# Two infini-attention and two Fourier layers: score blocks of 384 and 128 columns in one PSUM bank, value products merged, a 136-column memory update and direct row copies

## The chip, the cores and the metric

The kernel runs on one core of one Trainium2 chip. The metric is device time in microseconds (us) of one execution; of several runs the median counts. The engines are TensorE (PE in the profile, its weight loads PEld), VectorE (DVE), ScalarE (ACT), GpSimd (POOL) and SyncE (SP), which here only issues DMAs.

## The reference

Sequence 2048, width 512, 32 heads of 16, four segments of 512. Four residual layers alternate:

```python
def _A_ref(x, wq, wk, wv, wo, beta):          # q, k, v: x @ w, by head and segment
    for s in range(4):
        p = softmax(qs @ ks.T * scale + causal_mask);  a_dot = p @ vs
        a_mem = (phi(qs) @ M) / (phi(qs) @ z + 1e-6)
        outs.append(g * a_mem + (1 - g) * a_dot)
        M = M + phi(ks).T @ vs;  z = z + phi(ks).sum()
    return concat(outs) @ wo
def _B_ref(x, ...):                            # real part of a 2-D Fourier transform
    a, b = x @ dft_hid_re.T, x @ dft_hid_im.T
    return dft_seq_re @ a - dft_seq_im @ b
x = x + _A_ref(layernorm(x), ...); x = x + _B_ref(layernorm(x), ...)   # twice
```

## The kernel before

Large products are done as three fp16 products of split numbers (high and low half). A **group** is eight heads of one segment; there are 32 (`NGRP`): two layers, four segments, four groups. For each group, generators emit these steps:

- `s_p` and `s_v` project q, k and v. `t_split` splits q and k into halves (`hl`) and carries them as rows into the staging tiles `qst` and `kst`: two DMAs write `hl` to a DRAM tile `d`, four read it back with the rows rearranged. There are two such tiles of each (`NR` = 2), used in turn, so the rows of group i wait until the exponentiated scores of group i-2 are issued, `gate(("ST", i - NR))`.
- `s_x` computes scores to find each row's maximum. A head pair `p`, with its two halves `a` on the upper and lower 64 rows of the array at once, has four blocks of 128, 256, 384 and 512 columns (causal: block `t` has `128 * (t + 1)`). A **step** fills one PSUM bank for each half. `t_max` reduces each block on VectorE.
- `s_st` computes the scores again, transposed and with the maximum subtracted through two extra rows. `t_sel` exponentiates a whole bank on ScalarE into a tile `pt` and cuts the diagonal on GpSimd.
- `s_av` multiplies by the values. Four head pairs write four 32-row strips of one bank, in 32-column array strips side by side. The stationary operand is 32 fp32 columns of the value tile `vt`.
- `s_mem` reads the memory `macc` and updates it: `phk` (128 by 128, fp32) times `v[:, t]`, 192 fp32 columns (for each head pair the values of one head, 16 ones, the values of the other). `t_merge` joins both parts, `s_o` projects with `wo`; then `s_ab` and `s_f` do the Fourier layer, nearly all of it 128x512 fp16 products.

The order on every engine is set when the program is built. A list scheduler, `Plan`, keeps a cost model of the engines and always takes the generator that can go on first, corrected by a table of biases (`LEAN`). Every `yield need(engine, ...)` is a point where it may turn to another generator; instructions between two such points stay together. An engine then executes its instructions strictly in that order. TensorE works in three shapes: the whole array (m), two halves of 64 rows (h, the scores) and four strips of 32 columns (v, the value products). `t_warm` fills gaps that the planner foresees with dummy products of `onesb`. All instructions have the line of one helper (L272), so tiles tell them apart: `b` is a PSUM bank, `w`, `g`, `m` are work tiles, `y` the residual sum, which is also the staging area for weights at the start.

## Time and profile before

| | |
|---|---|
| median of three runs | 1695.57 us (1693.65 to 1700.11) |
| profiled execution, its own time | 1699.92 us |
| its span, first to last instruction | 1698.2 us |
| TensorE busy | 1662.3 us |
| VectorE, ScalarE, GpSimd busy | 1036.8, 872.3, 810.3 us |
| mean granted TensorE clock | 0.989 |

The span is what the trace covers; 1.7 us of the profiled time lie around it. A busy TensorE is not one that streams: the profile counts a product from its start to its modelled end, so the time in which one product drains and none streams is busy as well.

### The profile page before, as it was taken

The numbers are of one execution on the slowest core, as the hardware profiler recorded it, in microseconds if no ns is written. First come the engines' busy times: TensorE is split into PE (matmuls) and PEld (weight loads), VectorE is DVE, ScalarE is ACT, GpSimd is POOL, SyncE is SP. The second block draws the span as 40 slices with busy tenths as digits, with TensorE's granted clock in tenths as the row PEclk, the third lists the DMA queues.
The fourth block names the chain that finished last, engine by engine and source line by source line (L and its number), as shares of the span: only waits on it lengthen the run. The fifth ranks groups of instructions, "written<-read, shape, count | busy, mean of one in ns | idle before, by whom it ended". The sixth has DMA issues, their size and how long they took to land.

```text
span 1698.2 us, 32247 instructions
## 1 busy us (share of the span) xinstructions
PE 1662.3 (98%) x11145; PEld 734.7 (43%) x11145; DVE 1036.8 (61%) x3262; ACT 872.3 (51%) x1480; POOL 810.3 (48%) x1445
## 2 busy tenths in 40 slices
PE   8889999999999999999999999999999999999999
PEld 4344344444444344444544444443444444444444
DVE  8784865778677786635768558546575765433221
ACT  5487577755656666535376754655455325312000
POOL 4376556575565556634255644635454415322000
PEclk9789999999999999999999999999999999999999
DMA  7546545655357432525746663543435322131423
GB/s 182 147 116 178 128 132 159 172 142 152 94 148 208 126 119 84 189 56 196 193 148 187 182 179 90 132 116 98 140 91 149 105 85 76 57 125 38 143 70 123
DMA packets 208629, 222.92 MB, mean 131 GB/s; under 512 B 104520, under 2 KB 127048, under 8 KB 208464
## 3 DMA queue, kind: packets, MB, share of 16 engines
q1 hardware_dynamic: 208464, 220.85, 45.8%
q8 instruction: 88, 1.44, 0.4%
q14 instruction: 77, 0.63, 0.1%
HBM read 137.40 MB, written 61.87 MB: 117 GB/s over the span
## 4 chain that ended last, share of the span: by engine, by line
PE 77%; DVE 9%; ACT 5%; issue 4%; DMA 3%; POOL 2%; SPq 1%; ACTq 0%; DVEq 0%; POOLq 0%
PE b L272 77%; ACT w L272 4%; DVE junk L272 4%; SPq L272 1%; DVE w L272 1%; POOL w L272 1%; DMA w<-w 1%; DMA w<-x 1%; DVE m L272 1%; DVE mx L272 1%; DVE y L272 1%; DVE bst L272 0%; DVE cam L272 0%; DMA w<-in_cs_dram 0%; DVE pmax L272 0%
## 5 line engine op out<-in xcount | busy, mean ns | idle before, releaser
L272 PEld LDWEIGHTS <-w 128*128 128x128 f16 x5056 | 467.8, 98 | 612.8 <-issue 101.1
L272 PE MATMUL b<-w,w 128*128 128x512 f16 x3072 | 708.5, 380 | 1.7 <-DVE mx L272 0.8
L272 ACT ACTIVATE w<-b,fac 128x512 f32<-128x512 f32 (+1 forms) x728 | 419.2, 655 | 176.3 <-PE b L272 175.8
L272 DVE CUSTOM_DVE_ANT_0 junk<-b,cmask 128x128 bf16<-128x128 f32 (+3 forms) x1024 | 436.3, 483 | 71.6 <-PE b L272 71.1
L272 POOL TENSOR_TENSOR w<-w,w 128x512 f16<-128x512 f32 (+1 forms) x294 | 347.5, 1187 | 247.1 <-ACT w L272 223.6
L272 POOL TENSOR_SCALAR_AFFINE_SELECT w<-w 128x128 f32<-128x128 f32 (+2 forms) x704 | 237.0, 350 | 202.7 <-ACT w L272 194.1
L272 DVE SCALAR_TENSOR_TENSOR y<-b,fyu,y 128x512 f32<-128x512 f32 x200 | 148.9, 745 | 235.6 <-PE b L272 235.2
L272 ACT ACTIVATE w<-w,csc 128x512 f16<-128x512 f32 (+1 forms) x256 | 180.1, 720 | 41.5 <-DVE csc L272 32.8
L272 PE MATMUL b<-g,w 128*128 128x512 f16 x768 | 183.1, 383 | 3.2 <-DMA g<-w 0.8
L272 PE MATMUL b<-wd,w 128*128 128x512 f16 x768 | 176.8, 379 | 0.1
L272 PE MATMUL b<-w,vt 128*32 128x512 f32 (+3 forms) x2048 | 172.4, 449 | 1.9 <-POOL w L272 1.1
L272 ACT ACTIVATE w<-b 128x512 f16<-128x512 f32 x128 | 75.9, 596 | 189.4 <-PE b L272 179.3
L272 DVE SCALAR_TENSOR_TENSOR w<-b,w 128x512 f16<-128x512 f32 x128 | 87.6, 687 | 120.3 <-ACT w L272 118.7
L272 ACT ACTIVATE w<-w 128x512 f16<-128x512 f32 (+1 forms) x137 | 86.5, 632 | 90.1 <-DVE w L272 87.9
L272 PE MATMUL b<-kst,qst 48*128 48x128 f16 (+3 forms) x1024 | 117.5, 304 | 6.3 <-DVE mx L272 3.2
L272 PE MATMUL b<-qst,kst 50*128 50x512 f16 (+3 forms) x1024 | 115.8, 302 | 5.5 <-DVE mx L272 2.2
L272 PE MATMUL b<-w,g 128*128 128x128 f16 x1536 | 96.3, 221 | 0.0
L272 PEld LDWEIGHTS <-g 128*128 128x128 f16 x1536 | 89.6, 99 | 12.7 <-issue 7.8
L272 DVE STREAM_TRANSPOSE m<-b 128x512 f32<-128x512 f32 x112 | 75.6, 698 | 31.1 <-PE b L272 30.7
L272 PEld LDWEIGHTS b<-w,vt 128*32 128x32 f32 x2048 | 54.8, 110 | 87.7 <-issue 48.2
L272 PE MATMUL b<-wo,w 128*128 128x512 f16 x384 | 89.1, 379 | 0.0
L272 PEld LDWEIGHTS <-kst 50*128 50x128 f16 x1024 | 37.3, 94 | 111.7 <-issue 105.2
(105 smaller groups left out, 1019.3 us busy)
## 6 DMA issues: line engine op xcount, KB each, us to landing
w<-in_cs_dram SPq DMA_DIRECT2D x128, 256.0 KB, 3.5
cc<-w SPq DMA_DIRECT2D x128, 256.0 KB, 3.2
w<-cc SPq DMA_DIRECT2D x128, 256.0 KB, 3.1
w<-w SPq DMA_DIRECT2D x96, 256.0 KB, 3.5
d<-w SPq DMA_DIRECT2D x128, 128.0 KB, 2.5
w<-in_x_dram SPq DMA_DIRECT2D x32, 256.0 KB, 3.6
qst<-d SPq DMA_DIRECT2D x64, 128.0 KB, 2.7
kst<-d SPq DMA_DIRECT2D x64, 128.0 KB, 3.3
```

What stands on the lines that cost most here:

```text
L272: r = f(*args, **kw)
```

## The change

Five things, and a new order as their result.

1. **Steps.** The blocks of 384 and of 128 columns of a head pair share a bank, so a group has ten steps for each of its two score passes, not eleven. The order of steps is 512 first, then pairs of 256 and the shared ones (maxima, `"abc"`), or 512, shared, 256 (second pass, `"acb"`).
2. **Value products.** The products of the 384 and of the 128 columns follow each other without a scheduling point between them. The value tile is laid out as `[row, t, d, head]`, so the 32 stationary columns lie 8 fp32 numbers apart.
3. **Update.** The moving operand of the memory update is `v[:, t, :17]`: 128 value columns and 8 of ones, 136 for 192. The mask product reads it in two strided pieces.
4. **Rows.** For the first three groups, and whenever the tile's earlier user is already issued, q and k rows go straight from `hl` to the staging tile, by six DMAs. Three of the first groups have staging tiles of their own; the third lies in `y`.
5. **Scheduling points and engines.** In the first layer norm the scalar steps go to VectorE except the power, and its subtraction too. Dependent instructions on one engine get scheduling points between them. Costs and `LEAN` change, and dummy products no longer wait for the mask.

```diff
-        d = tc.dram_tile([2, 2, 64, 512], F16)
...
+        if i < DIRECT or prior[i] is not None and ("ST", prior[i]) in done:
+            if i == NR:
+                yield gate(*[("W", 2, g) for g in range(NG)])
+            for a in range(2):
+                o = dst[64 * a:64 * a + 64]
+                for r, j in ((0, 0), (16, 1), (32, 0)) if q else ((0, 0), (16, 0), (32, 1)):
+                    yield need("Y", hl)
+                    Y.dma_start(o[r:r + 16], hl[64 * a:64 * a + 64, j], est=(415, 520, 800))
...
-                mp = ps("pj", F32, (128, NP, 48))
+                mp = ps("pj", F32, (128, 17, HG))
                 for t in range(TT):
-                    T.matmul(mp, phk[:, 128 * t:128 * t + 128], v[:, t], start=(t == 0), stop=(t == TT - 1))
+                    T.matmul(mp, phk[:, 128 * t:128 * t + 128], v[:, t, :17], start=(t == 0), stop=(t == TT - 1))
...
+            a=[[(four, p, 0)] for p in range(NP)],
+            b=[[(two, p, 0), (two, p + 1, 256)] for p in range(0, NP, 2)],
+            c=[[(three, p, 0), (one, p, 384)] for p in range(NP)])
...
-                    for p in range(NP):
-                        T.matmul(av[32 * p:32 * p + 32, 128 * t:],
-                                 v[:, t, p].rearrange("k e d -> k (e d)")[:, 16 * a:16 * a + 32], tiles[p][1],
+                    for t in ts:
+                        for p in range(NP):
+                            T.matmul(av[32 * p:32 * p + 32, 128 * t:], v[:, t, :, NP * a + p], tiles[t, p][1],
...
+        if direct and STARTV:
+            yield need("V", mv)
+            V.tensor_scalar(mv[:, 2:3], mv[:, 1:2], 1e-5, 2.0 ** -20, op0=OP.add, op1=OP.mult)
+            yield need("G", mv)
+            G.tensor_tensor(rs, mv[:, 2:3], mhalf, op=OP.pow)
+            yield need("V", mv, rs)
+            V.tensor_scalar(mv[:, 3:4], mv[:, 0:1], rs, -1.0, op0=OP.mult, op1=OP.mult)
```

The order that results, at three places. TensorE, value products of the second group (the operand `vt_109`), in the kernel before: the 256-column products of the two halves, and then the 128-column ones, with scores (`kst`, `qst`) between.

```order
L272 MATMUL b_1526<-w_1595,vt_109 32x256 x2
L272 MATMUL b_1526<-w_1645,vt_109 32x256 x2
L272 LDWEIGHTS qst_106
L272 MATMUL b_1723<-kst_104,qst_106 128x512
L272 LDWEIGHTS qst_106
L272 MATMUL b_1724<-kst_104,qst_106 128x512
L272 MATMUL b_1548<-w_1596,vt_109 32x256 x2
L272 MATMUL b_1548<-w_1646,vt_109 32x256 x2
```

The same engine and group in the changed kernel: the 384 and the 128 columns of one half come from the same four tiles `w` and stand together.

```order
L281 MATMUL b_1561<-w_1545,vt_109 32x384
L281 MATMUL b_1561<-w_1556,vt_109 32x384
L281 MATMUL b_1561<-w_1613,vt_109 32x384
L281 MATMUL b_1561<-w_1649,vt_109 32x384
L281 MATMUL b_1561<-w_1545,vt_109 32x128
L281 MATMUL b_1561<-w_1556,vt_109 32x128
L281 MATMUL b_1561<-w_1613,vt_109 32x128
L281 MATMUL b_1561<-w_1649,vt_109 32x128
```

What moved: four kinds of value runs for a half of a group became three. Over the whole program the shape of the array changes 859 times in the order before and 760 times in the new one; ahead of the first output projection (first product with `wo`) it is 110 and 80.

VectorE at the start, layer norm of the first four tiles (`w_85` to `w_91`), before: the last of the four casts (`w_344`) follows the scales (`scl`, `inv`) of the first weights.

```order
L272 CAST w_319<-w_85 128x512
L272 CAST w_329<-w_87 128x512
L272 TENSOR_REDUCE amax<-y 128x1 x2
L272 TENSOR_SCALAR gmax<-b_365 128x2
L272 TENSOR_SCALAR gmax<-gmax 128x2
L272 TENSOR_SCALAR scl<-gmax 128x2
L272 TENSOR_SCALAR inv<-gmax 128x2
L272 CAST w_344<-w_91 128x512
```

After, same engine, the stretch that ends with the cast of the fourth tile (`w_450`).

```order
L281 TENSOR_REDUCE vm<-y 128x1 x4
L281 TENSOR_REDUCE amax<-vm 128x1
L281 TENSOR_TENSOR w_361<-w_89,w_361 128x512
L281 TENSOR_SCALAR mv<-mv,rs 128x1
L281 TENSOR_SCALAR gmax<-b_441 128x1
L281 TENSOR_SCALAR gmax<-gmax 128x1
L281 TENSOR_SCALAR scl<-gmax 128x1
L281 TENSOR_SCALAR inv<-gmax 128x1
L281 TENSOR_REDUCE amax<-y 128x1 x2
L281 CAST w_450<-w_91 128x512
```

What moved: the maxima of the value weights (`vm`) and of groups 1 and 2 of the q and k weights (`amax`) stand ahead of the fourth tile, and so do the subtractions of the first three tiles (`TENSOR_TENSOR`), which were GpSimd's.

SP's queue, rows of the first group's q (`w_490`) and k (`w_507`), before.

```order
L272 DMA d<-w_490 64x2x512 x2
L272 DMA d<-w_507 64x2x512 x2
L272 DMA qst_106<-d 32x2048
L272 DMA qst_106<-d 16x2048
L272 DMA qst_106<-d 32x2048
L272 DMA qst_106<-d 16x2048
L272 DMA kst_104<-d 16x2048
```

SP's queue after, where the third group's q rows (`w_829`) go to the third staging tile in `y`, right behind the first group's maxima (`mhl`).

```order
L281 DMA qst_106<-mhl 1x16x128 x4
L281 DMA w_132<-w_448 128x1024
L281 DMA y<-w_829 16x4x512 x6
L281 DMA w_1047<-in_x_dram 128x512
L281 DMA y<-d_282 2x2048 x2
```

What moved: the way through `d` is gone there, and the third group's rows wait for no earlier group. Of the 64 row sets 45 go direct; SP issues 1202 DMAs for 1200.

## Rows read from the trace of the kernel before

**Rows 1.** Page: busy time, share of the span, instructions of each engine.
```profile
PE 1662.3 (98%) x11145; PEld 734.7 (43%) x11145; DVE 1036.8 (61%) x3262; ACT 872.3 (51%) x1480; POOL 810.3 (48%) x1445
```

**Rows 2.** Windows view, five stretches: start, length, each engine's busy time, clock, DMA.
```profile
0.00:34.40 34.40, 28.30 (x215) 15.73 (x216) 30.16 (x90) 20.51 (x30) 17.01 (x31) 1.00 0.69 171
34.40:90.70 56.30, 50.66 (x314) 19.82 (x314) 43.11 (x172) 29.51 (x52) 22.93 (x42) 0.85 0.60 159
90.70:171.60 80.90, 74.25 (x611) 32.67 (x608) 54.01 (x215) 64.04 (x112) 57.66 (x108) 0.89 0.51 143
171.60:900.00 728.40, 719.66 (x4871) 317.67 (x4870) 494.42 (x1517) 446.11 (x746) 410.88 (x677) 1.00 0.51 145
900.00:1690.00 790.00, 785.12 (x5125) 347.06 (x5123) 414.34 (x1272) 312.10 (x543) 301.85 (x588) 1.00 0.40 114
```

**Rows 3.** Waits of TensorE: the longest in total, us, times, longest.
```profile
PE b L272 <- DVE mx L272: 10.6, 19, 1.6
```

**Rows 4.** Timeline of TensorE, two stretches: start, us, what.
```profile
138.71 2.10 PE L272 MATMUL b<-g,w 128*128 128x512 f16 x9
140.74 0.39 PE L272 MATMUL b<-qst,kst 50*128 50x512 f16 x2
141.06 0.82 PE L272 MATMUL b<-g,w 128*128 128x512 f16 x3
141.82 0.39 PE L272 MATMUL b<-qst,kst 50*128 50x512 f16 x2
...
1659.79 34.48 PE L272 MATMUL b<-w,w 128*128 128x512 f16 x159
```

**Rows 5.** Tile view of `vt`, products: ns least/median/most, first and last start.
```profile
L272 PE MATMUL b<-w,vt x2048: 272/486/1062, 62.7 to 1476.3; 128*32 128x512 f32 x47, 128*32 128x256 f32 x47, 128*32 128x128 f32 x47, 128*32 128x384 f32 x46
...
L272 PE MATMUL b<-vt,w x192: 326/326/430, 79.6 to 1260.2; 128*128 128x192 f32 x192
```

**Rows 6.** Timeline of TensorE: one update, one product of two columns.
```profile
25.80 0.28 PE L272 MATMUL b<-amax,ones 128*128 128x2 f32 x2
...
91.30 1.54 PE L272 MATMUL b<-vt,w 128*128 128x192 f32 x8 [0.21 <-ACT vt L272]
```

**Rows 7.** Groups by shape, weight loads: busy us, mean ns of one.
```profile
L272 PEld LDWEIGHTS b<-w,vt 128*32 128x32 f32 x2048 | 54.8, 110 | 87.7 <-issue 48.2 <-POOL w L272 23.4 <-DVE mx L272 3.0
L272 PEld LDWEIGHTS b<-vt,w 128*128 128x128 f32 x192 | 30.9, 190 | 10.7 <-issue 2.7 <-DVE mx L272 2.3 <-ACT vt L272 1.6
```

**Rows 8.** Timeline of TensorE: first q projection, first scores, first `wo` product.
```profile
16.88 1.46 PE L272 MATMUL b<-g,w 128*128 128x512 f16 x6 [0.68 <-ACT g L272]
...
34.39 0.62 PE L272 MATMUL b<-kst,qst 48*128 48x128 f16 x12
...
171.61 3.63 PE L272 MATMUL b<-wo,w 128*128 128x512 f16 x16
```

**Rows 9.** Groups by shape, VectorE.
```profile
L272 DVE TENSOR_REDUCE amax<-y 128x1 f32<-128x512 f32 x8 | 5.1, 673 | 0.0
...
L272 DVE TENSOR_TENSOR w<-w,w 128x512 f16<-128x512 f32 x2 | 2.1, 1062 | 5.8 <-ACT w L272 5.8
```

**Rows 10.** Timeline of VectorE: first and last maximum of the first group.
```profile
34.82 0.29 DVE L272 CUSTOM_DVE_ANT_0 junk<-b,cmask 128x128 bf16<-128x128 f32 x1 [0.88 <-PE b L272]
...
48.03 0.08 DVE L272 DVE_READ_ACCUMULATOR2_ANT mx<- 128x1 f32 x1
```

**Rows 11.** Timeline of TensorE: second group's maxima ready, third group's first scores, fourth's maxima ready.
```profile
69.74 0.39 PE L272 MATMUL b<-identf,mx 128*32 128x128 f32 x1 [1.56 <-DVE mx L272]
...
90.67 0.42 PE L272 MATMUL b<-kst,qst 48*128 48x128 f16 x8
...
131.24 0.27 PE L272 MATMUL b<-identf,mx 128*32 128x128 f32 x1 [0.94 <-ACT w L272]
```

**Rows 12.** Chain that ended last, ahead of those first scores: start, us, what.
```profile
83.43 2.35 DMA qst<-d
```

**Rows 13.** DMA issues: size, median us to landing.
```profile
d<-w SPq DMA_DIRECT2D x128, 128.0 KB, 2.5
```

More of the change, by code (lines that the diff above doesn't have):

```diff
@@ L46 @@
 AHEAD = 2
+XORDER, SORDER = "abc", "acb"
+DIRECT = 3
 NR = 2
@@ L83, in key @@
         f = self.fine.get(a.tensor.name)
+        if f and a.dtype == F16:
+            f *= 2
         return (a.tensor.name, a.offset // f) if f else a.tensor.name
@@ L176, in op @@
             c = n / 1.2 + (52 if src else 93) + (93 if any(a.free_size() == 1 for a in ins) else 0)
+            if name == "activation" and isinstance(kw.get("bias"), bass.AP):
+                c += 80
         elif eng == "V":
@@ L340, in body @@
     qst = [const.tile([128, NP, 512], F16, name=f"qst{i}") for i in range(NR)]
-    vt = [const.tile([128, TT, NP, 3, 16], F32, name=f"vt{i}") for i in range(NR)]
+    kst.append(y[:, 8:10, :].bitcast(F16).rearrange("p a (b n) -> p (a b) n", n=512))
+    qst.append(y[:, 10:12, :].bitcast(F16).rearrange("p a (b n) -> p (a b) n", n=512))
+    ring = [0, 1, 2] + [(i - 3) % 2 for i in range(3, NGRP)]
+    prior = [None] * 3 + [0, 1] + list(range(3, NGRP - 2))
+    vt = [const.tile([128, TT, 32, HG], F32, name=f"vt{i}") for i in range(NR)]
     identf = const.tile([128, 128], F32, name="identf")
@@ L415, in share @@
         A.activation(o[:, 0], src, AF.Copy, scale=s)
+        if YC:
+            yield need("A", o)
         A.activation(src, src, AF.Copy, scale=s)
@@ L418, in share, with view @@
         tt(o[:, 1], src, o[:, 0], OP.subtract)
+    def view(t, off, *dims):
+        return bass.AP(t.tensor, t.offset + off, [list(t.ap[0])] + [list(d) for d in dims])
     def flat(t):
@@ L558, in s_k @@
         bits(ra, 64, 1.0 / 64)
+        yield need("G", tag=("en", "pn"))
         cj = sb("en", F32, (128, 2, 4, 32))
@@ L601, in t_ln @@
         else:
+            if YL:
+                yield need("A", xi)
             A.activation(hl[:, 0], xi, AF.Copy)
-        yield need("VG", xi, hl)
-        tt(hl[:, 1], xi, hl[:, 0], OP.subtract)
+        if direct:
+            yield need("V", xi, hl)
+            V.tensor_tensor(hl[:, 1], xi, hl[:, 0], op=OP.subtract)
+        else:
+            yield need("VG", xi, hl)
+            tt(hl[:, 1], xi, hl[:, 0], OP.subtract)
         pl.close(xi)
@@ L692, in t_split @@
         done.add(("half", key))
+        i = key[1]
+        keep = kphi and not q
+        dst = (qst if q else kst)[ring[i]]
         yield need("Y", hl)
+        if i < DIRECT or prior[i] is not None and ("ST", prior[i]) in done:
+            if i == NR:
+                yield gate(*[("W", 2, g) for g in range(NG)])
+            for a in range(2):
[3 more added lines that the diff above has]
+                    Y.dma_start(o[r:r + 16], hl[64 * a:64 * a + 64, j], est=(415, 520, 800))
+            done.add(key)
+            if keep:
+                yield from t_kt(hl, kphi)
+            else:
+                pl.close(hl)
+            return
         d = tc.dram_tile([2, 2, 64, 512], F16)
@@ L696, in t_split @@
             Y.dma_start(d[a].rearrange("j p n -> p j n"), hl[64 * a:64 * a + 64], est=(651, 702, 467))
-        i = key[1]
-        if not kphi or q:
+        if keep:
+            spawn(t_kt(hl, kphi))
+        else:
             pl.close(hl)
-        elif i >= NR:
-            spawn(t_kt(hl, kphi))
-        if i >= NR:
-            yield gate(("ST", i - NR))
+        if i > NR:
+            yield gate(("ST", prior[i]))
         yield need("Y", d)
-        order = key[0] == "dq"
-        dst = (qst if order else kst)[i % NR]
         for a in range(2):
@@ L716, in t_split @@
         done.add(key)
-        if kphi and not q and i < NR:
-            yield from t_kt(hl, kphi)
     def t_kt(hl, kphi):
@@ L882, in together, with steps, t_max @@
         kinds.update(SHARED)
-    def t_max(sp, mx, a, p0, w, t, left):
-        n = 128 * (t + 1)
-        for p in range(p0, p0 + w):
-            o = (p - p0) * n
+    def steps(span):
+        one, two, four = (sorted(range(TT), key=lambda t: span(t)[1])[i] for i in (0, 1, 3))
+        three = 6 - one - two - four
+        return dict(
+            a=[[(four, p, 0)] for p in range(NP)],
+            b=[[(two, p, 0), (two, p + 1, 256)] for p in range(0, NP, 2)],
+            c=[[(three, p, 0), (one, p, 384)] for p in range(NP)])
+    XSTEP = steps(lambda t: (0, 128 * (t + 1)))
+    SSTEP = steps(lambda t: (128 * t, 512 - 128 * t))
+    def t_max(sp, mx, a, items, left):
+        for t, p, o in items:
+            n = 128 * (t + 1)
             yield need("V", sp)
@@ L1094, in t_c @@
         A.activation(cc[:, 0], raw, AF.Copy, scale=sc)
+        if YC:
+            yield need("A", cc)
         A.activation(raw, raw, AF.Copy, scale=sc)
@@ L1217, in t_warm @@
         at -= SPARE
-        if "CM" not in done or at - pl.free["T"] < IDLE or pl.lately(at) >= WARM:
+        if at - pl.free["T"] < IDLE or pl.lately(at) >= WARM:
             return
```

149 lines of the change are left out of this document (81 added, 68 removed).

## Prediction

> **What bounds the kernel now.** I read the page first: TensorE is busy for 1662.3 of 1698.2 us [rows 1]. That says where to look, not how much can be won, because a product that drains counts as busy. The windows come second. From 171.6 us to the end TensorE is busy for 99% of each stretch at full clock, while VectorE, ScalarE and GpSimd have room; ahead of that, in the first 171.6 us, it is busy less, twice at a mean clock of 0.85 and 0.89 (a mix of its two levels, 2.4 and 1.2 GHz), and VectorE is busy for 30.16 of the first 34.40 us [rows 2]. The waits come third: the longest cause of waiting for TensorE, the maxima, adds up to 10.6 us [rows 3]. So there are two stages. In the long one the time is what TensorE streams plus what it loses between streams. In the first, it is a chain through VectorE, the row DMAs and ScalarE.
>
> What streaming costs: 159 products of 512 columns in a row take 34.48 us, so one takes (34.48 - 0.38) / 158 = 0.2158 us. Nine of them between 138.71 and 140.74 should take 1.94 us and take 2.03; two scores side by side, 0.216 us, take 0.32 from 140.74 to 141.06; three, 0.65 us, take 0.76 up to 141.82 [rows 4]. Each change of the array's shape thus costs 0.09 to 0.11 us in which nothing streams; I use 0.095. With 859 changes that is some 82 us of the time before, and it is the price on which half of this change rests.
>
> **The update.** A pass with 192 fp32 columns lasts 326 ns, the shortest value pass, 128 columns, 272 ns [rows 5]. The difference, 54 ns for 64 columns, is 0.84 ns a column. 136 columns instead of 192 save 56 x 0.84 = 47 ns a pass. An update has eight passes [rows 6], there are 24 updates, and in the order five stand ahead of the first output projection. Behind it: 19 x 8 x 0.047 = 7.1 us. Lower bound nothing: a load of this operand takes 190 ns [rows 7], more than a short pass. But the eight passes with 192 columns already follow each other at (1.54 - 0.33) / 7 = 0.17 us, and two passes of two columns with loads of the same size stand in 0.28 us, less than twice 190 [rows 6]: loads overlap the passes and each other. I take 7.1. The two strided mask products on VectorE (48 in all) lie in a stage in which it is busy for 494 of 728 us [rows 2]; should they take twice as long, TensorE sees none of it, since a bank for the next projection is free meanwhile.
>
> **Ten steps for eleven, merged value products.** The columns stay the same. What goes is changes of shape: counted in the orders, 859 become 760, of which 749 and 680 stand behind the first output projection. 69 x 0.095 = 6.6 us. ScalarE has 64 instructions fewer in the second pass and the same columns, GpSimd 64 fewer cuts; both have cover [rows 2], and this is worth nothing by itself. Bounds: if the longer steps make TensorE wait for a bank somewhere, a few us go back; the order shows no gap, so I keep 6.6 as the value and 3 as the lower end.
>
> **Stationary columns 8 numbers apart.** Nothing in this trace loads a stationary operand with a step. A load of 32 fp32 columns takes 110 ns, one of 128 columns 190 [rows 7], so a column costs (190 - 110) / 96 = 0.83 ns and 32 of them 27 ns. A pass of 128 columns streams for 128 x 0.84 = 108 ns, about as long as a load; longer passes hide it. If the step doubles the price of a column, 27 ns are added where no pass hides them: two passes with each of the 64 half-group products of 128 columns, and the first load of each of the 99 value runs in the new order: (128 + 99) x 0.027 = 6.1 us. If it costs four times, 81 ns, 18 us. Lower end nothing. I take 3, half of the doubling.
>
> The Trainium skill speaks against this edit: "SBUF — State Buffer", Specifications (TRN2), says that SBUF lines are 16 bytes and that an access which touches a line only once does not reach full bandwidth. Every column of the new operand is on a line of its own, which would be the doubled case. No run so far shows it for TensorE.
>
> **The start.** Two things pull against each other. First, later: in the order the fourth layer-norm tile is cast after four further `amax` maxima and four `vm` maxima (0.67 us each), and three subtractions taken from GpSimd (1.06 each [rows 9]), with three rounds of scales behind them, some 1.3 us each: 8 x 0.67 + 3 x 1.06 + 3 x 1.3 = 12.5 us, the fourth subtraction 1.1 more. VectorE was nearly full there, so the first projection moves from 16.88 [rows 8] to about 30 us. The first scores need the q and k projection (24 products, 5.2 us), the split, and the last of twelve direct DMAs. Before they came 17.5 us after the first projection [rows 8]; without the trip through DRAM, whose write half lands after 2.5 us [rows 13], and without the weights of other groups in between, I put 13 to 14, so 43 us for 34.39.
>
> Second, earlier: the first group's maxima keep VectorE from 34.82 to 48.03 us, 13.3 us for a group [rows 10]. The second group's are ready at 69.74, but the third group's scores begin only at 90.67 [rows 11], because their rows waited for the first group's staging tile; the chain of waits shows that DMA at 83.43 [rows 12]. With a third tile and rows that are already there this 21 us gap is gone. Group by group: first maxima 44 to 59, second to 78, third to 95, fourth to 113, with 2 to 6 us of other VectorE work in each; before, the fourth's were ready at 131.24 [rows 11]. The output projection follows 40 us later, at 171.61 [rows 8]. That would be 18 us earlier. VectorE has 127.3 us of work in the 171.6 us [rows 2], and in the new order about 15 us more stand ahead (13 moved in at the start as above, the rest maxima of a later group), 142 in all, so it cannot be much before 155. I take 10 us earlier, with the same products of TensorE behind it: its work ahead of that point, and the passes of projections, are equal in both orders. Bounds: 4 us later to 20 earlier.
>
> **Sum.** 1699.92 (profiled time, span plus 1.7) - 7.1 - 6.6 - 10 + 3 = 1679.2. The median shown is 4.4 us below that execution, which would give 1674.9. I forecast 1677.
>
> **Rivals.** What can be told from no change is about 0.5%, 8.5 us either way: 1687.1 to 1704.
>
> *VectorE idles at the start as it did.* It stood idle for 44 of 171.6 us [rows 2]. If the new order leaves as much, its 142 us put the output projection at 186, 15 us later, and the time at 1699.9 - 13.7 + 15 + 3 = 1704, less 4 for the median: 1700. For it: the late first projection is certain. Against it: the gap at 70 to 90 us is the largest part of the idle time, and its cause is removed. A start that neither wins nor loses gives 1699.9 - 13.7 + 3 - 4 = 1685, and new waits of 5 us in the long stage 1690. All of these together: 0.25, most of it within 0.5%.
>
> *The strided load doubles.* 1677 + 3 = 1680, within the forecast case; four times, 1692, 0.1. By the Trainium skill's rule above the first would hold.
>
> *The strided load costs so much that it decides* (the other side). It has to eat 27 us over the forecast to end above 1704, with (128 + 99) places 0.12 us each: five times and more a column's price. At eight times, 27 x 7 = 190 ns, the 256-column passes (215 ns) no longer hide it either: 227 x 0.19 = 43 us plus 128 x 0.08 = 10, and 1677 - 3 + 53 = 1727. For it: nothing measured bounds the load. Against it: 32 columns are a quarter of a load that already hides behind other passes. 0.07.
>
> *The update does not get shorter* because its loads bind: 1677 + 7 = 1684. It is counted within the forecast case, a tenth of it.
>
> **How the numbers follow.** Forecast case 0.55 (1668 to 1686 by its bounds); start without gain, or new waits, 0.25; load four times 0.1; load that decides 0.07, a late start beyond its rival 0.03. The range takes in the start's 20 us early (1677 - 10 - 5) below and the rival at 1697 above: 1662 to 1697. Faster than 1687.1: 0.55 plus about half of the 0.25, 0.68; slower 0.09; between, 0.23.
>
> **What would show it.** Eight update passes at 0.116 us apart instead of 0.17; value loads still at 110 ns (right) or 137 and more (doubled); a first projection near 30, first scores near 43, third group's scores before 80 and the first `wo` product near 160; shape changes still 0.095 each. I am wrong if the first `wo` product comes after 172, or if value passes of 128 columns stand over 0.14 us apart.

## The result and the profile after

The changed kernel takes 1702.9 us in the median of 15 runs (1699.39 to 1708.69), the kernel before 1696.77 in 15 runs beside it. The ratio is 1.0041 with a 95% interval of 1.003 to 1.0052: slower by 7 us, just inside what the prediction called no change, and 26 us above the forecast. The profiled execution of the changed kernel has a span of 1703.8 us.

The page of the changed kernel, busy time, and its windows over the stretches of [rows 2].

```profile
PE 1655.0 (97%) x11150; PEld 753.3 (44%) x11150; DVE 1039.9 (61%) x3289; ACT 852.2 (50%) x1414; POOL 788.0 (46%) x1356
```

```profile
0.00:34.40 34.40, 23.43 (x102) 10.03 (x103) 29.18 (x95) 15.36 (x21) 10.61 (x19) 0.91 0.46 123
34.40:90.70 56.30, 46.37 (x294) 19.93 (x292) 43.01 (x165) 23.24 (x40) 16.47 (x28) 0.83 0.47 150
90.70:171.60 80.90, 73.55 (x611) 36.57 (x608) 58.74 (x230) 66.88 (x113) 59.68 (x107) 0.84 0.47 127
171.60:900.00 728.40, 717.46 (x4924) 327.31 (x4922) 488.02 (x1495) 435.99 (x718) 398.32 (x639) 1.00 0.47 139
900.00:1690.00 790.00, 784.25 (x5185) 355.15 (x5185) 419.04 (x1304) 310.73 (x522) 302.90 (x565) 1.00 0.37 109
```

TensorE is busy for 7.3 us less than before, and the span is 5.6 us longer [rows 1]: there is less to stream and more time in which nothing streams. The first two windows hold 9.2 us less of TensorE's work than those of [rows 2], and the clock is lower in the first three.

The tile view of `vt` (ns least/median/most), which answers to [rows 5, 7].

```profile
L281 PEld LDWEIGHTS b<-w,vt x2048: 135/139/178, 78.9 to 1501.1; 128*32 128x32 f32 x187
L281 PE MATMUL b<-vt,w x192: 279/279/596, 52.1 to 1324.4; 128*128 128x136 f32 x192
```

The update pass is 47 ns shorter, the figure forecast. The strided load is 29 ns longer, as forecast for the doubled case.

The timeline of TensorE, with the places of [rows 4, 6, 8, 11].

```profile
31.51 6.99 PE L281 MATMUL b<-g,w 128*128 128x512 f16 x24 [2.28 <-DVE bits L281]
...
47.63 0.60 PE L281 MATMUL b<-kst,qst 48*128 48x512 f16 x4
...
68.36 0.27 PE L281 MATMUL b<-identf,mx 128*32 128x128 f32 x1 [1.13 <-DVE mx L281]
...
88.63 0.39 PE L281 MATMUL b<-identf,mx 128*32 128x128 f32 x1 [2.26 <-DVE mx L281]
...
99.69 0.62 PE L281 MATMUL b<-y 48*128 48x512 f16 x3
...
149.47 0.28 PE L281 MATMUL b<-identf,mx 128*32 128x128 f32 x1
...
191.58 2.10 PE L281 MATMUL b<-wo,w 128*128 128x512 f16 x9
...
225.46 2.12 PE L281 MATMUL b<-w,w 128*128 128x512 f16 x9
227.51 0.39 PE L281 MATMUL b<-kst,qst 48*128 48x384 f16 x4
...
230.52 1.19 PE L281 MATMUL b<-vt,w 128*128 128x136 f32 x8
```

The first projection comes at 31.51 us and the first scores at 47.63; the first group's maxima are ready at 68.36, the second group's at 88.63, 19 us later than before, the fourth's 18, and the first output projection 20 [rows 8, 11]. Nine products of 512 columns still take 0.11 us more than 1.94 when a change of shape follows, and eight update passes take 1.19 us where they took 1.54 [rows 6].

The timeline of VectorE at the start, and that of SP's queue ahead of the third group's first scores.

```profile
7.26 0.69 DVE L281 BATCH_NORM_STATS2 bst<-w 128x6 f32<-128x512 f32 x1
...
10.55 0.17 DVE L281 BATCH_NORM_AGGREGATE mv<-bst 128x2 f32<-128x6 f32 x1
...
17.00 2.46 DVE L281 TENSOR_REDUCE vm<-y 128x1 f32<-128x512 f32 x4
...
19.56 1.68 DVE L281 TENSOR_TENSOR w<-w,w 128x512 f16<-128x512 f32 x1
21.16 0.20 DVE L281 TENSOR_SCALAR mv<-mv,rs 128x1 f32<-128x1 f32 x1
...
22.97 0.42 DVE L281 CAST w<-w 128x512 f16<-128x512 f32 x1
...
30.68 0.68 DVE L281 COPY g<-b 128x1024 f16<-128x1024 f16 x1
```

```profile
72.17 4.51 SPq L281 DMA_DIRECT2D y<-w  x6
...
89.22 1.31 SPq L281 DMA_TRANSPOSE g<-w  x1
90.64 2.47 SPq L281 DMA_DIRECT2D qst<-mhl  x4
93.14 3.80 SPq L281 DMA_DIRECT2D y<-w  x6
```

The fourth tile's statistics start at 7.26, but its scalar leaves VectorE at 21.16, behind the maxima of the value weights. On SP the third group's k rows (the second `y<-w`) stand behind the second group's maxima and a transposing DMA, and leave from 93.14 on: the third tile was free and the rows were not there.

One account serves all that follows. **Streamed** is what TensorE's products take at full clock: for each product of a trace its columns at 2.4 GHz, which with 0.0025 us each gives the 0.2158 us of 512 columns [rows 4]; fp32 columns twice, which gives the 0.116 us from one update pass of 136 columns to the next in the trace; two halves or four strips at once divided by two or four; dummy products left out. The 96 products that read the memory (`macc`) run two at a time as well, 7 ns apart in the trace, and are counted whole here: streamed is some 20 us too high and lost as much too low, by the same amount in every row. **Changes** of the array's shape are counted in the trace, at 0.095 us. **Lost** is the rest of the span: waits, low clock, loads that nothing hides.

```
us                       span   streamed  changes      lost    (to 60, 60-200, from 200)
before                 1698.2     1519.6  859: 81.6    97.0     28.3   43.0   25.7
changed                1703.8     1510.7  760: 72.2   121.0     33.1   57.4   30.5
```

The parts gave back 8.9 + 9.4 us, and 24.0 us more were lost, 19.2 of them before 200 us. Up to 8 of the 24 go with the lower clock: over the first three stretches, length times the missing share of the clock is 25.6 us here and 17.3 in [rows 2]. The experiments ask why more is lost.

### The profile page after: what moved, and what is told of

It reads as the page before. It is cut to its first block, busy times and chain, and to the rows that moved or that the text cites. A ratio compares the mean times of both kernels' runs of the same rounds, so it can differ in the third digit from the quotient of the medians.

```text
span 1703.8 us, 32170 instructions
## 1 busy us (share of the span) xinstructions
PE 1655.0 (97%) x11150; PEld 753.3 (44%) x11150; DVE 1039.9 (61%) x3289; ACT 852.2 (50%) x1414; POOL 788.0 (46%) x1356
## 4 chain that ended last, share of the span: by engine, by line
PE 80%; DVE 6%; ACT 4%; DMA 3%; issue 3%; SPq 2%; POOL 2%; ACTq 0%; POOLq 0%; DVEq 0%
PE b L281 80%; ACT w L281 4%; DVE junk L281 2%; SPq L281 2%; DMA w<-w 2%; POOL w L281 1%; DVE w L281 1%; DMA w<-in_cs_dram 0%; DVE mx L281 0%; DVE bst L281 0%; DMA w<-x 0%; DVE y L281 0%; POOL wd L281 0%; DMA w<-in_x_dram 0%; DVE pmax L281 0%
## 5 line engine op out<-in xcount | busy, mean ns | idle before, releaser
L281 ACT ACTIVATE w<-b,fac 128x512 f32<-128x512 f32 x664 | 408.2, 693 | 172.2 <-PE b L281 167.3
L281 DVE CUSTOM_DVE_ANT_0 junk<-b,cmask 128x512 bf16<-128x512 f32 (+3 forms) x1024 | 438.3, 484 | 81.1 <-PE b L281 80.8
L281 POOL TENSOR_TENSOR w<-w,w 128x512 f16<-128x512 f32 (+1 forms) x286 | 337.5, 1188 | 240.1 <-ACT w L281 220.1
L281 POOL TENSOR_SCALAR_AFFINE_SELECT w<-w 128x256 f32<-128x256 f32 (+1 forms) x640 | 227.1, 362 | 249.4 <-ACT w L281 237.6
L281 ACT ACTIVATE w<-w,csc 128x512 f16<-128x512 f32 (+1 forms) x256 | 174.6, 722 | 45.0 <-DVE csc L281 39.5
L281 PE MATMUL b<-kst,qst 48*128 48x512 f16 (+1 forms) x992 | 108.5, 303 | 6.0 <-DVE mx L281 4.1
L281 PE MATMUL b<-qst,kst 50*128 50x512 f16 (+1 forms) x992 | 109.1, 304 | 5.2 <-DVE mx L281 2.6
L281 PEld LDWEIGHTS b<-w,vt 128*32 128x32 f32 x2048 | 69.8, 144 | 82.1 <-issue 58.0
L281 DVE TENSOR_REDUCE cam<-w 128x1 bf16<-128x512 f32 x128 | 81.0, 678 | 11.4 <-DMA w<-in_cs_dram 11.4
```

The costliest lines, as they stand in the source:

```text
L281: r = f(*args, **kw)
```

## Experiments on the late start

My theory was that the late fourth layer-norm tile makes everything late by 20 us; the rivals were the strided load, and the steps or the planner's order elsewhere. In the expectations this is the first theory; the second blames the ten steps, the third the direct rows, the fourth the planner's order as a whole. Times are medians; a ratio is that to the kernel before, run beside it, with its 95% interval.

**Neighbouring stationary columns, same order.** The value tile by head; the mask product and the host's layout of the value weights follow.

```diff
-    vt = [const.tile([128, TT, 32, HG], F32, ...
+    vt = [const.tile([128, TT, HG, 32], F32, ...
-  T.matmul(av[32 * p:32 * p + 32, 128 * t:], v[:, t, :, NP * a + p], tiles[t, p][1], ...
+  T.matmul(av[32 * p:32 * p + 32, 128 * t:], v[:, t, NP * a + p], tiles[t, p][1], ...
```

> The changed kernel with the value tile laid out by head, so that the 32 stationary columns are neighbours again; the order of every engine is that of the changed kernel, instruction by instruction, and the update still moves 136 columns. If the start costs the time (first theory), the value loads fall from 139 to 110 ns and the time by 3 to 6 us below the changed kernel, with the first output projection still near 191 us. If the strided load is what eats the gain (rival), the time falls by 15 us or more. If the step is harmless because the loads hide, by less than 2 us.

Measured 1703.37 us, ratio 1.0034 (1.002 to 1.0047); loads back at 110 ns. Against the changed kernel's ratio that is 1 us of gain with 3 either way. The strided load is not where the gain went, and a first output projection at 189 says the same.

**Scalars of the first layer norm on GpSimd.**

```diff
-STARTV, YL, YB, YM, YC, YS = 1, 1, 1, 1, 1, 1
+STARTV, YL, YB, YM, YC, YS = 0, 1, 1, 1, 1, 1
```

> The changed kernel with the scalar steps of the first layer norm back on GpSimd; the tensor subtractions stay on VectorE. First theory (the late fourth layer-norm tile is what makes the start 20 us later): the fourth BN_AGGR stands ten instructions earlier on VectorE, the first projection comes near 20 to 26 us for 31.5, the first output projection at 178 to 186 for 191.6, and the time falls by 6 to 12 us. Rival (the start is limited by the sum of VectorE's work, in whatever order): first projection earlier, first output projection still at 188 or later, time within 3 us of the changed kernel.

Measured 1720.68, ratio 1.0138 (1.0115 to 1.0161). The first projection comes at 24.75 us, the first output projection at 187.90, and by the ratios the kernel is 16 us slower than the changed one. Neither side expected that.

**The layer norm's generator as before.**

```diff
-        if direct and STARTV:
-            yield need("V", mv)
-            V.tensor_scalar(mv[:, 2:3], mv[:, 1:2], 1e-5, 2.0 ** -20, op0=OP.add, op1=OP.mult)
...
+        yield need("G", mv)
+        G.tensor_scalar(mv[:, 2:3], mv[:, 1:2], 1e-5, 2.0 ** -20, op0=OP.add, op1=OP.mult)
...
```

> The changed kernel with the layer-norm generator exactly as it was before the change: scalars on GpSimd, subtractions where the planner puts them, no added scheduling points in it. The first ten-step groups, direct rows, third staging tile, merged value products and 136-column update stay. First theory: first projection back at 16 to 20 us, first scores at 30 to 36, first output projection at 160 to 175, and the time 15 to 25 us below the changed kernel, that is below the kernel before. It has 813 changes of the array's shape for 760, all but 13 behind the first output projection, which gives 4 us back. Rival (the loss sits in the score steps and the planner's new order): first projection early and the first output projection still behind 185, time within 4 us of the changed kernel.

Measured 1716.59, ratio 1.0114 (1.0095 to 1.0134). The timeline of its TensorE: first projection, second group's maxima, first output projection.

```profile
16.40 1.46 PE L281 MATMUL b<-g,w 128*128 128x512 f16 x6 [0.68 <-ACT g L281]
...
86.34 0.28 PE L281 MATMUL b<-identf,mx 128*32 128x128 f32 x1 [0.52 <-DVE mx L281]
...
189.33 2.75 PE L281 MATMUL b<-wo,w 128*128 128x512 f16 x12
```

The first projection is where it was in the kernel before, to half a microsecond, and at 86 us the second group's maxima are nearly as late as in the changed kernel again. This felled my theory: an early start is lost within 70 us, in another place. The rival had the late output projection right, but not the time, which is 12 us above the changed kernel by the ratios.

**All six switches off.**

```diff
-STARTV, YL, YB, YM, YC, YS = 1, 1, 1, 1, 1, 1
+STARTV, YL, YB, YM, YC, YS = 0, 0, 0, 0, 0, 0
```

> The changed kernel with all six switches of the fifth edit off: no added scheduling points between dependent instructions and scalars on GpSimd, but the first layer norm's subtractions still on VectorE and the new biases. First theory: the fourth layer-norm tile is early (its BN_AGGR at the place it had before), first projection 18 to 24 us, first output projection 165 to 178, time 12 to 20 us below the changed kernel, with 797 shape changes. Rival (sum of VectorE's work): first output projection at 185 or later and the time within 4 us of the changed kernel. If the added points themselves help the long stage, the stretch behind the first output projection gets longer by a few us.

Measured 1707.49, ratio 1.0066 (1.0049 to 1.0084), first projection at 23.37 and first output projection at 193.64, and a time 4 us above the changed kernel by the ratios, as the rival had it. The same lesson.

## Experiments on the parts, each alone on the kernel before

**The update alone.** Value tile by head as above, `v[:, t, :, :17]` as moving operand. To make room, the mask is bf16 and the small tiles `mx`, `mhl` and `rc` have half their buffers, as in the change.

```diff
-                mp = ps("pj", F32, (128, NP, 48))
+                mp = ps("pj", F32, (128, HG, 17))
-  T.matmul(mp, phk[:, 128 * t:128 * t + 128], v[:, t], ...
+  T.matmul(mp, phk[:, 128 * t:128 * t + 128], v[:, t, :, :17], ...
```

> The kernel before with one part of the change: the update over 136 columns. The value tile is laid out by head, so that the stationary columns stay neighbours; everything else, biases too, as before. By the update theory of the prediction: 24 x 8 passes 47 ns shorter, 9.0 us, of which 7.1 behind the first output projection, and 7 changes of the array's shape fewer, 0.7 us: 7 to 10 us below the kernel before, first output projection still near 171 us. Rival (loads of the update's operand bind, or the planner's new order eats it): within 3 us of the kernel before.

**The ten steps alone**, with the merged value products; generators as in the change, old value tile and update.

```diff
-            for t in range(TT):
-                n = 128 * (t + 1)
-                w = 512 // n
-                for p0 in range(0, NP, w):
+            for items in [x for k in XORDER for x in XSTEP[k]]:
```

> The kernel before with one part of the change: ten steps for eleven, 512 first, and merged value products; value tile, update of 192 columns, row copies, layer norm and biases as before. 814 changes of shape for 859: by the prediction 4.3 us below the kernel before. If the ten steps are what makes the changed kernel lose 15 to 20 us between 140 and 250 us (second theory: longer steps, the 512 columns first, leave TensorE nothing between two maxima), the first output projection comes at 180 or later and the time is 8 us or more above the kernel before.

**The direct rows alone**, with the third tile.

```diff
+        if i < DIRECT or prior[i] is not None and ("ST", prior[i]) in done:
...
+                    Y.dma_start(o[r:r + 16], hl[64 * a:64 * a + 64, j], est=(415, 520, 800))
```

> The kernel before with one part of the change: rows straight to the staging tiles by six DMAs for the first three groups and where the earlier user is issued, third staging tile in y; steps, update, layer norm and biases as before. If the row copies make the changed kernel late (third theory: six issues of about 0.6 us on SP in place of two and four, and the third tile that waits until the first weights are used), the first output projection comes at 180 or later and the time is 8 to 20 us above the kernel before. If they do what the prediction took them to do, the third group's scores start before 80 us, the first output projection comes near 160, and the time is 5 to 15 us below the kernel before.

**Update and steps together.**

```diff
+            for items in [x for k in XORDER for x in XSTEP[k]]:
...
+  T.matmul(mp, phk[:, 128 * t:128 * t + 128], v[:, t, :, :17], ...
```

> The kernel before with the update over 136 columns and the ten steps with merged value products, stationary columns neighbours; row copies, layer norm, scheduling points and biases as before. 781 changes of shape for 859. If neither of the two is to blame, 9.0 + 7.4 us: 12 to 18 us below the kernel before, first output projection at 172 or earlier. If the ten steps are to blame, 180 or later and no gain over the kernel before.

Measured, in this order: 1716.06, ratio 1.0117 (1.0097 to 1.0137); 1715.54, 1.0113 (1.0094 to 1.0132); 1717.10, 1.0128 (1.0109 to 1.0147); 1704.89, 1.0053 (1.0038 to 1.0068). Each part alone makes the kernel slower, by 19 to 22 us, and the first two together by 9. The update's 192 passes are shorter in its run (278 ns in the median), 8.9 us less are streamed, and 25.7 us more are lost. None of the four gave the time that the prediction's terms give it. The output projection comes at 183.64, 190.22, 172.97 and 177.94 us; only the ten steps alone did what the theory that blames them expected, and update and steps with other biases, below, speak against that theory. Parts that each save work, each cost 20 us, and do not add up point to what they share: each makes the planner lay out a new order, with biases made for the old one.

## Experiments on the order

**The update in the order of before.** The planner is told the costs of 192 columns; the order of every engine is that of the kernel before, row by row.

```diff
             n, w = out[0].free_size(), aps[1]
+            n = 192 if n == 136 else n
```

> The update over 136 columns as in the run with the update alone, but the planner is told the costs of 192 columns, so that every engine has the order of the kernel before, instruction by instruction. Fourth theory (the parts are worth what the prediction gave them, and the loss is that of a new order for which the biases were not made): 24 x 8 passes 47 ns shorter, 9.0 us: 7 to 10 us below the kernel before, first output projection at 169 to 172. Rival (the shorter update itself uncovers a wait): within 3 us of the kernel before, or above it as the run with the update alone was.

Measured 1694.17, ratio 0.9988 (0.9979 to 0.9996): 22 us better than the same instructions in their own order, but 2 us better than the kernel before and not 9. Most of the loss of the update alone is thus its order; the small gain is the rival's number. The profiled spans, 1690.8 and 1698.2 us, differ by more because the profiled execution of the kernel before lies 3 us above its median; I go by the ratio, and an account from one execution is good to some 4 us.

**The order alone.** Nothing but the planner's idea of one cost.

```diff
             n, w = out[0].free_size(), aps[1]
+            n = 136 if n == 192 else n
```

> The reverse: every instruction of the kernel before, with 192 columns, but the planner is told that the update costs what 136 columns cost. No instruction is added, removed or resized; about a third of the rows of the order stand elsewhere. Fourth theory: 8 to 25 us above the kernel before, without any change of work. Rival (the order is worth little and each part brought its own loss): within 4 us of the kernel before.

Measured 1731.10, ratio 1.0203 (1.019 to 1.0216): **34 us slower with the same work**, more than the 8 to 25 expected. What the planner itself chooses differs a little with the order: 25 more dummy products, and eight operations on VectorE that GpSimd had (one went the other way). Its windows over the stretches of [rows 2]:

```profile
0.00:34.40 34.40, 27.96 (x211) 15.59 (x212) 30.43 (x90) 20.52 (x30) 17.28 (x31) 1.00 0.69 170
34.40:90.70 56.30, 50.79 (x319) 19.84 (x316) 43.47 (x172) 28.96 (x50) 22.16 (x40) 0.85 0.58 158
90.70:171.60 80.90, 71.85 (x540) 29.58 (x544) 56.41 (x224) 66.88 (x117) 59.12 (x110) 0.87 0.51 142
171.60:900.00 728.40, 711.45 (x4711) 314.96 (x4704) 472.44 (x1433) 423.42 (x705) 393.56 (x644) 1.00 0.48 139
```

The first 90 us are nearly those of before. Then TensorE gets through fewer products: 540 for 611 in the third stretch, 4711 for 4871 in the fourth. No single wait does it; the account above gives 31.6 us lost more than before, 11.5 of them between 60 and 200 us and 19.8 behind.

**The changed kernel without direct rows.** All rows through DRAM, two staging tiles.

```diff
-DIRECT = 3
+DIRECT, LATER = 0, 0
-        if i < DIRECT or prior[i] is not None and ("ST", prior[i]) in done:
+        if i < DIRECT or LATER and prior[i] is not None and ("ST", prior[i]) in done:
```

> The changed kernel without the fourth edit: all rows by way of the DRAM tile, two staging tiles; steps, update, layer norm, points and biases as changed. Its order is again one for which the biases were not made. Fourth theory: above the changed kernel by 3 to 20 us. Third theory (the direct rows cost by themselves, by six issues of about 0.62 us on SP for two and four of about 0.45): at or below the changed kernel, 1695 to 1703.

Measured 1709.05, ratio 1.0077 (1.006 to 1.0094), 6 us above the changed kernel, as the order theory had it.

**Update and steps with other biases.** The table was chosen by trying variants of it at build time and keeping that with which the planner's own plan ends first. Beside this the kernel is that of update and steps together.

```diff
-LEAN = dict(... s_memV=40.0, ... t_mergeY=-150.0, ... t_cY=80.0, t_lnG=80.0, ... t_phiA=150.0, ... s_wA=-150.0, ...)
+LEAN = dict(... s_memV=150.0, ... t_mergeY=-40.0, ... t_lnG=150.0, ... t_phiA=-80.0, ... s_wA=40.0, ... s_memT=300.0, ...)
```

> The kernel with the update of 136 columns and the ten steps alone (neighbouring stationary columns, rows through DRAM, layer norm as before, 4.9 to 9 us slower than the kernel before with its biases), instruction for instruction the same work, but with another table of biases, chosen so that the planner's own plan ends earlier. Fourth theory: the 16 us that update (9.0) and shape changes (63 fewer, 6.0) are worth appear, 1675 to 1685, 20 to 30 us below the run with the old biases, and faster than both kernels. Rival (the ten steps cost what they save): within 5 us of the run with the old biases, 1700 to 1710.

Measured **1675.35, ratio 0.988 (0.9867 to 0.9893)**: 29 us faster than the same work with the old table, and faster than both kernels.

**The kernel before with a table chosen likewise.**

```diff
-LEAN = dict(... t_cY=80.0, ... t_splitV=-40.0, t_phiA=150.0, ... t_mergeV=150.0, ...)
+LEAN = dict(... t_cY=-80.0, ... t_phiA=40.0, ... t_mergeV=80.0, ... s_ldY=40.0)
```

> The kernel before, every instruction as it was, with a table of biases chosen in the same manner as that of the fastest run so far (plan of its own that ends earlier), so another order. If that run owes its 20 us to update and ten steps (parts theory), this one stays within 8 us of the kernel before, 1687 to 1702. If it owes them to a better table alone (rival), this one comes down as far, 1673 to 1683.

Measured 1694.57, ratio 0.9986 (0.9977 to 0.9996): 2 us. One other table, found in the same way, does not give the kernel before the 20 us, as the parts theory expected. They are not all of the parts either: the fast order with 192 columns, below, is 13 us faster than this run (0.9909 against 0.9986), of which 60 fewer changes of shape make 5.7; the rest is less lost in that order.

**The changed kernel with a table chosen likewise.** `t_lnG` stays at -300.

```diff
-LEAN = dict(... t_mergeA=40.0, ... s_kV=-300.0, ... s_lnY=-150.0, ... t_abV=300.0, ... t_phkV=80.0, ...)
+LEAN = dict(... t_mergeA=150.0, ... s_kV=-150.0, ... s_lnY=300.0, ... t_phkV=300.0, ... t_selG=-150.0, s_memT=40.0)
```

> The changed kernel, direct rows, third tile and strided value load included, with a table chosen in the same manner. If direct rows and the fifth edit are harmless and only the order was at fault, it ends near the fastest run, 1672 to 1684. If the direct rows cost by themselves (third theory), it ends at 1688 or later although its plan is as short.

Measured 1685.71, ratio 0.9938 (0.9924 to 0.9952): the changed kernel's work, 17 us faster, between the two expected ranges. In this order 37 of the 64 row sets go direct, for 45. Its first projection and first output projection, from the timeline of TensorE:

```profile
16.93 1.24 PE L281 MATMUL b<-g,w 128*128 128x512 f16 x5 [0.90 <-ACT g L281]
...
174.09 2.12 PE L281 MATMUL b<-wo,w 128*128 128x512 f16 x9
```

So the late start was of the order too, not of the fifth edit, which is all in this run but for its biases.

**The same without direct rows**, table chosen likewise.

```diff
-DIRECT = 3
+DIRECT, LATER = 0, 0
-LEAN = dict(... s_wV=80.0, ... t_mergeY=-150.0, ... t_lnG=-300.0, ... t_resV=-80.0, ...)
+LEAN = dict(... s_wV=-40.0, ... t_mergeY=40.0, ... t_lnG=150.0, ... t_resV=300.0, ...)
```

> The changed kernel without the fourth edit (all rows through DRAM, two staging tiles), table chosen in the same manner; strided value load, layer norm on VectorE and points as changed. If direct rows cost by themselves: 1676 to 1686, and 8 us or more below the run with direct rows and new biases. If they do not: within 5 us of that run.

Measured 1685.72, ratio 0.9943 (0.9926 to 0.9959). Equal within 4 us, each in an order of its own: no gain or cost of direct rows and third tile is seen here beyond that.

**What update and stride are worth in a good order.** Three runs, each in the order of another, row by row: the run of 1675.35 us with the old value tile and 192 columns; the same with the strided value tile; and the last run with neighbouring columns.

```diff
-  T.matmul(mp, phk[:, 128 * t:128 * t + 128], v[:, t, :, :17], ...
+  T.matmul(mp, phk[:, 128 * t:128 * t + 128], v[:, t], ...
```

> The fastest run so far in its own order, instruction by instruction, but with the update of 192 columns and the value tile of the kernel before; the planner is told the costs of 136. If an update pass is worth its 47 ns wherever the order is good, it is 7 to 10 us slower than the fastest run, 1682 to 1686, ratio to the kernel before 0.992 to 0.995. If the update is worth the 2 us that the same edit gave in the order of before, 1676 to 1679.

```diff
-    vt = [const.tile([128, TT, HG, 32], F32, ...
+    vt = [const.tile([128, TT, 32, HG], F32, ...
```

> The fastest run so far in its own order, instruction by instruction, but with the value tile of the change, so that the 32 stationary columns lie 8 numbers apart. If the doubled load of the prediction (6 us) shows where TensorE seldom waits for anything else: loads 139 ns for 110, and 4 to 7 us slower than the fastest run, ratio to the kernel before 0.990 to 0.993. If nearly all of it hides, as in the order of the changed kernel (about 1 us in the medians): 0.987 to 0.989.

```diff
-    vt = [const.tile([128, TT, 32, HG], F32, ...
+    vt = [const.tile([128, TT, HG, 32], F32, ...
```

> The run without direct rows and with new biases, in its own order, instruction by instruction, but with neighbouring stationary columns: the reverse of the last edit, on another order. Doubled load visible: 4 to 7 us faster than that run, ratio to the kernel before 0.990 to 0.992. Hidden: within 2 us of it. What then still separates it from the fastest run is the fifth edit (layer norm on VectorE, added points, costs) and what the two tables differ in, which no run here takes apart.

Measured 1681.29, ratio 0.9909 (0.9892 to 0.9925): the update is worth 4.9 us (0.9909 - 0.988), 3.5 either way, between the two expected. 1675.47, ratio 0.9873 (0.9859 to 0.9886): the stride costs -1 us, 3 either way. 1683.18, ratio 0.9916 (0.9902 to 0.993): the stride costs 4.6 us there, 3.6 either way. With the first experiment's 1 us the three prices of the stride are 1, -1 and 5 us.

The account for the runs that decide:

```
us                       span   streamed  changes      lost    (to 60, 60-200, from 200)
e3  layer norm as before 1714.4   1510.7  813: 77.2   126.5     32.7   58.4   35.4
e5  update alone         1714.3   1510.7  852: 80.9   122.7     28.8   55.9   38.0
e9  the same, old order  1690.8   1510.7  859: 81.6    98.5     28.7   44.9   25.0
e10 order alone          1731.0   1519.6  872: 82.8   128.6     28.6   54.5   45.5
e8  update and steps     1702.7   1510.7  781: 74.2   117.8     28.8   54.3   34.6
e12 the same, new biases 1674.1   1510.7  796: 75.6    87.8     28.9   37.3   21.6
e13 before, new biases   1690.8   1519.6  856: 81.3    89.8     24.5   41.9   23.4
e14 changed, new biases  1683.5   1510.7  780: 74.1    98.7     31.6   42.8   24.3
```

Streamed and changes differ by 18 us at most between any two rows; what is lost differs by 41. Among these runs the order decides more than the work.

## Why the prediction was wrong

**The update** was right in its mechanism: 47 ns a pass, and passes 0.116 us apart in the trace. Its size was not all passed on: 8.9 us less to stream became 2.0 us in the order of before and 4.9 in the best order. A possible cause stands in the last section.

**Ten steps and merged products.** 859 changes became 760, at the price forecast: in the trace of the changed kernel they are 90 to 96 ns (medians by the two shapes), as before. The best run has 60 changes fewer than the kernel before with a fitting table, 5.7 us. What ScalarE's and GpSimd's missing instructions were worth by themselves no run shows.

**Stationary columns 8 apart.** Loads of 139 ns for 110 are the doubled case: 29 ns where 27 were reckoned. By the Trainium skill, "SBUF — State Buffer", Specifications (TRN2), lines of 16 bytes that are touched once do not give full bandwidth; the traces agree, at 0.9 ns a column. In time it is 1, -1 and 5 us, about the 3 that the sum had.

**The start is the step that failed**, and its -10 us became a loss: the first output projection came 20 us later, 24.0 us more were lost. Two parts of its working held. The first projection came at 31.5, forecast about 30; and VectorE's work ahead of the output projection was 140.5 us, forecast 142. What did not hold is that the gap of 21 us between the second group's maxima and the third group's first scores goes with a third tile, because the rows are already there. The prediction put the whole gap down to the tile [rows 11, 12]. The trace of the kernel before shows that most of it was not the tile's. VectorE makes the second half of every group's q and k rows; the third group's are its fifth and sixth, and they come behind the second group's maxima of 69.74 us.

```profile
70.67 0.67 DVE L272 SCALAR_TENSOR_TENSOR w<-b,w 128x512 f16<-128x512 f32 x1
...
71.98 0.69 DVE L272 SCALAR_TENSOR_TENSOR w<-b,w 128x512 f16<-128x512 f32 x1
```

```profile
72.97 2.63 SPq L272 DMA_DIRECT2D d<-w  x4
```

These four DMAs are issued by 75.60 and land some 2.5 us later [rows 13]; the rows are read back from 83.43 us on. So the tile can have held them for some 5 us at most. The changed kernel still has the third group's k rows behind the second group's maxima, now of 88.63 us, on VectorE (the first of two such products) as on SP, which they leave from 93.14 on:

```profile
90.76 1.28 DVE L281 SCALAR_TENSOR_TENSOR w<-b,w 128x512 f16<-128x512 f32 x2
```

The gap went from 21 us to 11, and the stages ahead of it were late as well: the first group's maxima were ready at 68.36 for 59, the second's at 88.63 for 78, and the third group's first scores came at 99.69 instead of before 80. The prediction rests on the q rows, which stand right behind the first group's maxima in SP's order; the k rows do not. The rival that VectorE idles at the start as it did gave 1700 us and an output projection at 186; it came out at 1702.9 and 191.6, and VectorE idled for 51 us where it had 44. It had a quarter of the chances, together with others, and its mechanism is close to what happened.

But the wrong step had a wrong assumption below it: that a new order, apart from the places I looked at, costs nothing. The runs show what stands in its place. The work of the kernel before in an order disturbed by one number takes 34 us more (e10). The changed kernel's work with another table takes 17 us less than with the table it has (e14), and then all the parts together are 10.5 us faster than the kernel before (12.9 to 8.1); the terms of the sum without the start were -7.1 - 6.6 + 3 = -10.7. That these agree so closely is in part luck, since the update brought less than its term. The forecast's direction was that of the parts; the result is that of the order.

What stays open: which of the rows of the changed order costs most. The late start alone does not, since repairing it alone gave other orders, none faster, and no run moves the third group's k rows alone. Also open is what separates the changed kernel with new biases (1685.7) from update and steps alone (1675.4): stride (-1 to 5 us), fifth edit and the fit of the two tables were not taken apart.

## What to carry to other kernels

Where a planner writes the order from a table of biases, a change of a cost or an instruction can be a new order as well, and here ten such orders, the changed kernel's among them, ended 7 to 34 us above the kernel before, against 5 us (the update) to 20 (update and steps) that edits gave in an order that fitted them. So measure an edit in an unchanged order first (tell the planner the old costs), and compare kernels only with a table chosen anew for each. In a forecast, the new order is a term of its own; the trace of the old order did not bound it here. And a gap between two stages is not the work of the last wait in it: read from the trace when the operands were made.

## What the runs showed of the hardware

With the shorter passes the granted clock was lower in one order, and not so in every pair. The windows from 60 to 200 us in one order, three kernels: 136 columns, 192 columns, and 136 with the strided load.

```profile
60.00:200.00 140.00, 130.34 (x985) 58.16 (x985) 103.55 (x377) 103.88 (x175) 94.92 (x167) 0.91 0.54 143
```

```profile
60.00:200.00 140.00, 128.25 (x980) 58.55 (x979) 103.11 (x371) 102.42 (x172) 93.12 (x166) 0.94 0.56 139
```

```profile
60.00:200.00 140.00, 128.41 (x994) 59.16 (x992) 104.27 (x378) 105.77 (x178) 95.51 (x169) 0.95 0.56 148
```

The mean granted clock there is 0.91, 0.94 and 0.95, a mix of 1.2 and 2.4 GHz, and over the timed runs the median clock of the whole span is 0.9915, 0.995 and 0.995. The pair in the order of before shows the same, 0.990 with 136 columns for 0.992. A mean clock 0.0035 lower over 1675 us is 2 x 0.0035 x 1675 = 12 us more at half clock, in which up to 6 us less is streamed. This could cover the 4 us that the shorter update fails to give in the best order. But the third kernel has the same shorter passes at 0.95, and its time is that of the first (1675.47 and 1675.35): either its longer loads take what its clock gives back, or the clock is worth little here. That shorter passes are the cause of the lower clock is thus not shown. The Trainium skill, "TensorE: Matmul & The Clock Gate", Part 1, says that the half clock is the default and activity releases it. The first two kernels agree, in that the one with less to stream has the lower clock (0.91 for 0.94); the third, with as little to stream and 0.95, does not.

Six direct row DMAs took SP 3.80 and 4.51 us to issue, 0.63 and 0.75 us each, as the rows from SP's queue show.
